# A new list of work and a finer planner's clock for a fused attention and maxout kernel

## Chip, cores and metric

The kernel runs on one core of a Trainium2 chip. The metric is the device time of one execution in microseconds (us): before, 318.02 us, the median of three runs (317.68 to 318.27).

## What is computed

Two stages in one program. First an attention through 32 inducing vectors, for four batches of 12544 rows of 128; then a maxout layer over all 50176 rows: two products to 1024 columns, their elementwise maximum, and a product back to 128.

```python
def mab(q, kv):
    s = scale * (q @ kv.transpose(0, 2, 1))
    s = s - s.max(-1, keepdims=True)
    a = np.exp(s)
    a /= a.sum(-1, keepdims=True) + 1e-09
    return a @ kv
h = mab(I, x)              # I: inducing, (B, 32, 128); x: (B, 12544, 128)
x2 = mab(x, h)             # (B, 12544, 128), then flattened to (50176, 128)
h1 = x2 @ w1               # 128 x 1024
h2 = x2 @ w2
out = np.maximum(h1, h2) @ w_out   # 1024 x 128
```

## The kernel before

**The algebra.** max(h1, h2) is h1 + relu(h2 - h1). The second attention's output is e2 times h, divided by a denominator per row, so both products are folded into the 32-row h: `hwd` is h times (w2 - w1) and `m1` is h times w1 times w_out. What is left per row is e2 (32 exponentials), a product of e2 with `hwd` (contraction over 32), a relu, a product of the relu with w_out (contraction over 1024, eight pieces of 128) and a product of e2 with `m1`, summed in the same PSUM bank; the eviction divides by the denominator.

**Tiling.** A batch has 98 chunks of 128 rows. A block is four quarters (one for each group of 32 rows of the TensorE array) of up to four chunks, 28 blocks in all. A quarter gives 2 x width units; a unit is 512 columns of relu. A quarter's chunks are also one output group, 108 in all, each with a PSUM bank while it is summed.

**Modes of TensorE.** It works in three ways: full (128 x 128: final matmuls with w_out at L932, small products), row (four tiles of 32 rows: units and the linear term, L1085) and column (four tiles of 32 columns: staging at L657, pooled scores at L356, pooled sums at L414).

**The list of work.** Every engine's order is written out by hand (`tc.manual_schedule`). `ORDER` (L1113) is a list of words, executed one after the other when the program is built:

- `pN.F`: a row phase (L1031) of up to N units, of different quarters, plus one group's linear term if N is under 4 and one is due; each unit's relu is then evicted by ACT (L1102) or by DVE (L1105), whichever would end first by the planner's clock; a bit of F turns the choice round for one unit
- a number: so many final matmuls (L920), in the order of the groups; with a group's last one the group is evicted (L954) by DVE, or chunk by chunk by ACT where `EVICT` has a 1, and stored on SP's queue (L989)
- `s`: the next block is staged (L643): its exponentials e2, evicted by ACT (L669)
- `xB.j`: a DMA transpose of a piece of batch B (L205), on SP; `gK`: a DMA transpose of block K's e2 on SP, and its denominators summed and inverted on POOL (L703); a block whose turn has not come by its first final gets its denominators by small matmuls instead (L749, L764)
- `cB.u`, `tB.u`, `aB.u`, `rB`: batch B's scores with the inducing vectors (ACT's exp, L369), their transpose on SP (L395), and the weighted sums (L398); the last `a` issues the loads of the next batch on POOL (L195)
- `eB`, `hB`, `wB`, `mB`: the small products to h, `hwd` and `m1` of batch B
- `H1`, `W`: second half of batch 0's `hwd`, and w1 times w_out

**The planner's clock.** `Clock` (L21) follows the engines with fixed durations while the list is executed. It picks the PSUM bank that comes free first (L172), the engine of a relu, and whether to put warming matmuls ahead of a wait (L879). It does not run on the chip.

**The head.** Batch 0 is loaded in twelve parts, transposed on TensorE, scored and summed in the order of `HEAD` (L814). The difference w2 - w1 is taken in three pieces (L572), w1 is cast to f16 in two halves (L576) and transposed on TensorE (L585).

**Tiles.** PSUM banks are tiles of a pool with a tag for each bank (L172); the relus have two buffers a quarter (L746), outputs six buffers (L957).

Of the kernel before, what the change touches and what calls it, by code (L numbers as in the profile page):

```python
# [20 lines left out]
class Clock:  # L21


    PAIR = 0.0558
    SWITCH = {"full": 0.11, "row": 0.097, "col": 0.097}
    LAT = 0.20
    ROW = 0.224
    SEM = 0.05

    def __init__(self):  # L30
        self.pe = self.act = self.dve = self.sp = 0.0
        self.pool = self.loading = self.loaded = 0.0
        self.stored = [0.0] * NOUT
        self.issue, self.tile = 0.0, [0.0] * 4
        self.mode = "full"
        self.bank = [0.0] * 8
        self.idle = {}
        self.log = []
        self.busy = {}
# [7 lines left out]
    def run(self, us, mode="full", ready=0.0, why="data"):  # L47
        if mode != self.mode:
            self.pe += self.SWITCH[mode]
            self.busy["sw"] = self.busy.get("sw", 0) + self.SWITCH[mode]  # L50
            self.mode = mode
# [5 lines left out]
    def on_act(self, ready, us, tail=0.12):  # L57
# [3 lines left out]
    def on_dve(self, ready, us, tail=0.085):  # L61
# [3 lines left out]
    def on_sp(self, ready, us=1.33):  # L65

        start = max(self.sp, ready)
        loading = start < 41.0 or self.loading - 1.0 < start < self.loaded - 1.0
        self.sp = start + us + (2.0 if loading and us > 1.5 else 0.0)
        late = 0.0  # L70
        if start < 42.0:
            late = 39.5 + 0.35 * (start - 27.85)
        elif start > self.loading - 1.0:
            late = min(start + 8.6, self.loaded + 4.7)
        return max(start + us + 2.4, late)
# [56 lines left out]
def kernel(  # L132
# [28 lines left out]
    relup = ctx.enter_context(tc.tile_pool(name="relup", bufs=2))  # L161
    outp = ctx.enter_context(tc.tile_pool(name="outp", bufs=NOUT))
# [7 lines left out]
    uid = [0]  # L170

    def bank(shape, dtype=F32, only=None):  # L172
        i = min(range(8), key=lambda j: ck.bank[j]) if only is None else only
        uid[0] += 1
        return i, psum.tile(shape, dtype, name=f"ps{uid[0]}", tag=f"bank{i}", bufs=1)
# [14 lines left out]
    def load_x(b, i, after=None):  # L190
# [5 lines left out]
        if b:  # L196
            if i == 0:
                ck.loading = ck.pe
            ck.on_pool(ck.pe, 0.55)
            st[b]["ld", i] = ck.loaded = ck.pe + 8.0 + 2.75 * i if b > 1 else 26.2 + 2.5 * i  # L200
# [4 lines left out]
    def transpose_x_dma(b, j):  # L205
# [3 lines left out]
        landed = ck.on_sp(st[b]["ld", i], 1.7 if n == 7 else 2.6)  # L209
# [4 lines left out]
    head16 = relup.tile([128, 4096], F16, name="head", tag="relu3")  # L214
# [10 lines left out]
    wf = relup.tile([128, 4096], F16, name="wf", tag="relu0").bitcast(F32)  # L225
    w1f, w2f = wf[:, 0:J], wf[:, J : 2 * J]
    w1s = relup.tile([128, 4096], F16, name="w1s", tag="relu1")
# [7 lines left out]
    repd = consts.tile([128, 128], F32, name="repd")  # L235
    pace = consts.tile([128, 1], F32, name="pace")

    with tc.manual_schedule(engines={ET.PE, ET.DVE, ET.Activation, ET.Pool, ET.SP}):

        xf = relup.tile([128, 4096], F16, name="xf", tag="relu2")[:, 0 : 256 * P1].bitcast(F32)  # L240
# [14 lines left out]
        nc.gpsimd.dma_start(out=woutp, in_=moe_w_out.rearrange("(jb j) c -> j jb c", j=128))  # L255
        nc.vector.memset(warm, 0.0)
# [9 lines left out]
        LANDED = [0.0, 7.58, 9.72, 11.95, 13.05, 14.12, 16.27, 17.37, 18.31, 18.94, 19.26, 19.57]  # L266
# [20 lines left out]
        def p1_scores(b, i):  # L287
# [14 lines left out]
            else:  # L302
                at = 1024 + 2 * M * (i % 2)
                et = head16[:, at : at + 2 * M].rearrange("p (k m) -> p k m", m=M)
            nc.scalar.activation(out=et[:, 0:n, :], in_=ps[:, 0 : n * M], func=AF.Exp, scale=scale)
            ck.bank[bi] = ck.on_act(end, 0.05 + n * M / 1200.0)
            st[b]["et", i] = et, ck.bank[bi]

        def p1_accum(b, i, lo=0, hi=P1):
# [4 lines left out]
            if b == 0:  # L314
                last = i == len(parts[0]) - 1
                ck.wait(ready, "p1")
                for j in range(lo, hi, 4):
                    m = min(4, hi - j)
                    nc.tensor.matmul(  # L319
                        out=st[0]["eps"][0 : m * M, 0:1],  # L320
                        lhsT=et[:, j : j + m, :].rearrange("p k m -> p (k m)"),
                        rhs=ones16[:, 0:1],
                        start=(i == 0 and j == 0),
                        stop=(last and j + m == n),
# [10 lines left out]
                st[0]["end"] = ck.run(0.0285 * (hi - lo) + 0.015 * ((hi - lo + 3) // 4))  # L335
# [866 lines left out]
```

## Time and profile before

| what | value |
| --- | --- |
| median of three runs | 318.02 us |
| the profiled execution: its own time | 317.76 us |
| its span, first to last instruction | 316.0 us |
| granted TensorE clock | 0.998 |
| final matmuls L932 | 3136, 203.5 us busy |
| row matmuls L1085 | 1262 |
| relus on ACT (L1102), on DVE (L1105) | 470 and 314, 241.0 and 199.7 us busy |
| evictions on DVE (L964) | 103, 66.0 us busy |
| last TensorE instruction ends at | 312.93 us |
| DMA, share of 16 engines: SP's and other hardware queues, POOL's | 55.8%, 22.4% |

Busy time of a matmul is modelled and overlaps that of the next; where the text speaks of what a matmul costs, it is the interval from its start to the start of the next instruction. "Issue" as a releaser means that the profile shows nothing that was waited for. The profile is of one execution, so sums are made against its own 317.76 us.

### The profile page before, as it was taken

The numbers are of one execution on the slowest core, as the hardware profiler recorded it, in microseconds if no ns is written. First come the engines' busy times: TensorE is split into PE (matmuls) and PEld (weight loads), VectorE is DVE, ScalarE is ACT, GpSimd is POOL, SyncE is SP. The second block draws the span as 40 slices with busy tenths as digits, with TensorE's granted clock in tenths as the row PEclk, the third lists the DMA queues.
The fourth block names the chain that finished last, engine by engine and source line by source line (L and its number), as shares of the span: only waits on it lengthen the run. The fifth ranks groups of instructions, "written<-read, shape, count | busy, mean of one in ns | idle before, by whom it ended". The sixth has DMA issues, their size and how long they took to land.

```text
span 316.0 us, 12577 instructions
## 1 busy us (share of the span) xinstructions
PE 308.6 (98%) x5308; PEld 239.9 (76%) x5308; DVE 274.5 (87%) x488; ACT 280.2 (89%) x580; POOL 125.8 (40%) x187
## 2 busy tenths in 40 slices
PE   6998999999999999999999999999999999999996
PEld 3885777777877777778877787887868777788885
DVE  2468999999878999988999899989899889999885
ACT  3669999999999999998999989899999999998891
POOL 7363060666620066067510064674406564461500
PEclk9999999999999999999999999999999999999999
DMA  8999999989799999898499999897323233324232
GB/s 203 208 252 205 207 219 146 207 229 230 127 218 245 245 183 174 190 233 207 121 225 252 213 227 215 204 174 203 106 85 118 100 106 118 119 88 140 102 120 101
DMA packets 81336, 55.81 MB, mean 177 GB/s; under 512 B 62816, under 2 KB 66176, under 8 KB 81280
## 3 DMA queue, kind: packets, MB, share of 16 engines
q1 hardware_dynamic: 75312, 41.32, 55.8%
q0 software_dynamic: 5968, 13.70, 22.4%
q8 instruction: 41, 0.67, 0.9%
q14 instruction: 15, 0.12, 0.1%
HBM read 27.28 MB, written 25.69 MB: 168 GB/s over the span
## 4 chain that ended last, share of the span: by engine, by line
PE 94%; DMA 2%; ACT 1%; DVE 1%; issue 1%; POOL 0%; POOLq 0%
PE ps L932 60%; PE ps L1085 23%; DMA xn<-in_x_dram 2%; PE ps L657 2%; PE ps L356 2%; PE ps L414 2%; PE ps L276 1%; PE ps L328 1%; PE ps L292 1%; PE ps L521 0%; DVE relu L1105 0%; PE ps L319 0%; ACT e L669 0%; DVE o L964 0%; ACT e_first L696 0%
## 5 line engine op out<-in xcount | busy, mean ns | idle before, releaser
L1102 ACT ACTIVATE relu<-ps 128x512 f16<-128x512 f32 x470 | 241.0, 627 | 17.5 <-PE ps L1085 16.5
L1105 DVE TENSOR_SCALAR relu<-ps 128x512 f16<-128x512 f32 x314 | 199.7, 684 | 20.6 <-PE ps L1085 19.0
L932 PE MATMUL ps<-woutp,relu 128*128 128x128 f16 x3136 | 203.5, 219 | 0.2
L932 PEld LDWEIGHTS <-relu 128*128 128x128 f16 x3136 | 176.6, 98 | 34.4 <-issue 28.7
L1085 PE MATMUL ps<-e,hwd 32*128 32x512 f16 (+2 forms) x840 | 82.8, 361 | 0.1
L720 POOL TENSOR_TENSOR half<-ed 128x256 f32<-128x256 f16 (+2 forms) x23 | 14.1, 613 | 145.8 <-DMA ed<-e 145.8
L724 POOL TENSOR_TENSOR rd<-den,minus 128x16 f32<-128x16 f32 (+2 forms) x23 | 60.7, 2639 | 1.8
L964 DVE TENSOR_TENSOR o<-ps,rd 128x512 f32<-128x512 f32 (+3 forms) x83 | 53.2, 643 | 3.9 <-PE ps L1085 2.8
L1085 PE MATMUL ps<-m,e 32*128 32x128 f16 x372 | 36.8, 216 | 0.0
L1085 PEld LDWEIGHTS <-hwd 32*128 32x128 f16 x880 | 26.7, 91 | 12.8 <-issue 3.8
L1085 PEld LDWEIGHTS <-e 32*128 32x128 f16 x372 | 22.4, 92 | 10.4 <-issue 2.7
L720 POOL TENSOR_TENSOR half<-half 128x32 f32<-128x32 f32 (+3 forms) x69 | 22.3, 323 | 5.4
L195 POOL DMA_DIRECT2D xn<-in_x_dram x32 | 17.6, 563 | 5.7 <-DMA xn<-in_x_dram 4.3
L280 DVE COPY xT<-ps 128x512 f16<-128x512 f16 (+3 forms) x12 | 5.7, 485 | 8.6 <-PE ps L276 8.6
L964 DVE TENSOR_TENSOR o<-ps,rp 128x512 f32<-128x512 f32 (+3 forms) x20 | 12.8, 642 | 0.0
L369 ACT ACTIVATE eu<-ps 128x512 f16<-128x512 f32 x18 | 11.0, 617 | 0.6 <-PE ps L356 0.3
L669 ACT ACTIVATE e<-ps 128x512 f16<-128x512 f32 (+2 forms) x21 | 11.1, 607 | 0.3 <-PE ps L657 0.2
L283 ACT COPY xT<-ps 128x768 f16<-128x768 f16 (+3 forms) x10 | 5.7, 574 | 4.3 <-PE ps L276 4.2
L276 PE MATMUL ps<-identity,xn 128*128 128x128 f16 x98 | 7.6, 220 | 1.4 <-DMA xn<-in_x_dram 0.9
L657 PE MATMUL ps<-xT,hT 128*32 128x512 f16 (+3 forms) x110 | 8.1, 361 | 0.1
L276 PEld LDWEIGHTS <-xn 128*128 128x128 f16 x98 | 5.5, 97 | 2.9 <-DMA xn<-in_x_dram 1.2
L356 PE MATMUL ps<-xT,inducingT 128*32 128x512 f16 x72 | 6.8, 386 | 0.0
(110 smaller groups left out, 117.7 us busy)
## 6 DMA issues: line engine op xcount, KB each, us to landing
out_dram<-o SPq DMA_DIRECT2D x90, 256.0 KB, 3.0
xn<-in_x_dram POOLq DMA_DIRECT2D x24, 448.0 KB, 10.4
out_dram<-o SPq DMA_DIRECT2D x10, 128.0 KB, 2.9
wf<-in_moe_w_dram POOLq DMA_DIRECT2D x4, 256.0 KB, 6.0
xn<-in_x_dram POOLq DMA_DIRECT2D x4, 224.0 KB, 10.2
xT<-xn SPq DMA_TRANSPOSE x33, 4.4
xf<-in_x_dram SPq DMA_DIRECT2D x1, 512.0 KB, 3.7
xf<-in_x_dram SPq DMA_DIRECT2D x1, 384.0 KB, 4.2
```

What stands on the lines that cost most here:

```text
L195: nc.gpsimd.dma_start(out=xn_at[b, i][:, 0:n, :], in_=xr[b, :, k0 : k0 + n, :])
L276: nc.tensor.transpose(ps[:, j, :], xn[:, g + j, :], identity16)
L356: nc.tensor.matmul(out=ps[32 * g : 32 * (g + 1), :], lhsT=inducingT, rhs=xT_tiles[b % 2][:, U * u + 4 * g : U * u + 4 * (g + 1), :], start ...
L657: nc.tensor.matmul(out=ps[32 * q : 32 * (q + 1), 128 * t : 128 * (t + n)], lhsT=hq, rhs=xT[:, c : c + n, :], start=True, stop=True, tile_p ...
L669: nc.scalar.activation(out=blk.e2[:, 0 : 128 * wd], in_=ps[:, 0 : 128 * wd], func=AF.Exp, scale=st[0]["rs"] if blk.b == 0 else scale,)
L720: nc.gpsimd.tensor_tensor(out=dst, in0=cur[:, :, 0:n], in1=cur[:, :, n : 2 * n], op=ALU.add)
L724: nc.gpsimd.tensor_tensor(out=rp[:, 0:wd, :].rearrange("p t q -> p (t q)"), in0=den[:, 0 : 4 * wd], in1=minus1[:, 0 : 4 * wd], op=ALU.pow,)
L932: nc.tensor.matmul(out=g.ps[:, 128 * c : 128 * (c + 1)], lhsT=g.blk.relu[g.q][:, 128 * (jb * w4 + t) : 128 * (jb * w4 + t + 1)], rhs=woutp ...
L964: nc.vector.tensor_mul(osb[:, 0:m, :], g.ps[:, 0 : m * C].rearrange("p (s c) -> p s c", s=m), g.blk.rp[:, t0 : t0 + m, q : q + 1].broadcas ...
L1085: nc.tensor.matmul(**seq.pop(0))
L1102: nc.scalar.activation(out=dst, in_=src, func=AF.Relu)
L1105: nc.vector.tensor_scalar(out=dst, in0=src, scalar1=0.0, scalar2=None, op0=ALU.max)
```

## The change

The list of work is another, and the relu of each unit now names its engine. The planner's clock gets other durations and more detail. The order in which the head's transposes, scores and sums run, and the order of the loads among themselves, stay; some of the small work between them moves:

- `ORDER` and `EVICT` are new. In `pN.V` a bit of V now means DVE, no bit ACT. `H` is the second half of `hwd` alone, the new word `V` holds all transposes of w1 and their copies (their first half stood ahead of the list, their second in `H`). There is a word `nK` for finals in column mode; the list does not use it.
- A unit is given only when the piece of `hwd` that it needs has been issued.
- Columns 256 to 512 of w2 - w1 move from DVE to POOL, between the loads of batch 1; the second half of w1's cast moves from ACT to POOL.
- The denominators of batch 0's pooling are summed over pieces of 4, 4, 3, 3 chunks in place of 4, 4, 4, 2, and the two last parts of two chunks together.
- Seven transfers of a few bytes from the second part of x to an unused corner of a relu buffer are issued on SP behind the loads.
- The PSUM banks are slices of one tile, the relus of a quarter slices of one tile, the outputs slices of one tile.

```diff
 class Clock:
-    PAIR = 0.0558
-    SWITCH = {"full": 0.11, "row": 0.097, "col": 0.097}
+    PAIR = 0.0563
+    COLS = 0.0566
+    SWITCH = {
+        "full": {"row": 0.095, "col": 0.095},
+        "row": {"full": 0.082, "col": 0.088},
+        "col": {"full": 0.1, "row": 0.094},
+    }
+    STEP = 0.0035
 ...
-    ROW = 0.224
+    ROW = 0.2226
 ...
+    psall = psum.tile([128, 8, 512], F32, name="psall", tag="psall")
+    relus = [big.tile([128, 2, 4096], F16, name=f"relus{q}", tag=f"relus{q}") for q in range(4)]
+    relu1 = [big.tile([128, 1024], F16, name=f"relu1_{q}", tag=f"relu1_{q}") for q in range(2)]
+    osbs = big.tile([128, NOUT, 4, C], F32, name="osbs", tag="osbs")
 ...
+        for i, k in enumerate((8, 12, 14, 15, 4, 2, 1)):
+            nc.sync.dma_start(out=probe[0:k, 16 * i : 16 * i + 8 + i], in_=xn_at[0, 1][0:k, 0, 0 : 8 + i])
 ...
+        SUMS = {14: ((0, 4), (4, 4), (8, 3), (11, 3)), 7: ((0, 4), (4, 3)), 6: ((0, 3), (3, 3)), 4: ((0, 4),)}
 ...
-        for i in range(7):
-            if i == 3:
-                difference(nc.gpsimd, 512, J, 22.4, 1.2)
+        load_x(1, 0)
+        difference(nc.vector, 0, 256, 21.0, 0.34)
+        difference(nc.gpsimd, 256, 512, 21.0, 0.64)
+        load_x(1, 1)
+        load_x(1, 2)
+        difference(nc.gpsimd, 512, J, 22.9, 1.25)
+        cast_w1(1)
+        for i in range(3, 7):
             load_x(1, i)
-        difference(nc.vector, 0, 256, 21.0, 0.3)
         sums = small_h(0)
-        difference(nc.vector, 256, 512, 21.0, 0.3)
-        weights_2(0)
 ...
-        cast_w1(1)
-        weights_2b(0)
 ...
             unit = blk.units[q][u]
+            if ("hw", ((unit[3] + 1) * (4 // unit[2]) - 1) // 2) not in st[blk.b]:
+                return None
 ...
-                if (max(ck.act, ready) + 0.477 <= max(ck.dve, ready) + 0.597) != bool(flip >> k & 1):
+                relu_out(q, blk, unit, bi, ready, bool(vector >> k & 1))
```

The list, old and new:

```diff
-s p4.13 s H1 W g2 p4.1 p2 8 m0 4 p3 p2.1 10 p3 p2 13 p3.2 6 p4.5 22 p2 p4.8 17 x1.0 p4.8 4 g1 11
-p4.1 13 p4.9 p1 16 p3.4 p2 14 p4.10 6 x1.1 4 x1.2 x1.3 x1.4 x1.5 x1.6 2 p3.6 s s s s 6 g3 6 p4.5
-14 x1.7 1 x1.8 p4.8 19 p4.10 p2.1 12 x1.9 5 p3 14 p4.4 c1.0 15 p1 p4.5 14 p4.3 g4 13 p4.8 25 p4.6
-p3.2 10 x1.10 17 p2 p3.1 15 c1.1 p4.2 12 t1.1 2 p3 6 p4.2 4 g5 11 c1.2 c1.3 p4.1 18 p4.4 t1.3 21
-p3.5 p3 22 c1.4 p1.1 p4.1 19 p2 p4.8 5 g6 21 p4.2 p2 c1.5 19 r1 a1.1 p3.2 p4 t1.5 19 a1.3 p4.9
-p2.2 29 p3.3 p4 26 p4.1 a1.5 5 p3.1 p2.3 1 e1 11 p4.12 1 h1 17 w1 s s s s p3.2 19 m1 15 p4.6 p3.6
-30 p3.1 p3.3 24 p3 p3.3 27 p3.2 p3.1 20 p4.3 p2 15 s p4.1 18 p2.1 p3 15 g7 g8 7 p3.3 p4.2 9 g9 12
-x2.0 3 x2.1 x2.2 s p1.1 p4.4 x2.3 12 p4.5 14 p4.6 14 p4 14 p3 21 p3.6 p4.8 14 g10 4 x2.4 4 x2.5
-x2.6 9 p4.13 s c2.0 14 p4.6 p1 5 x2.7 4 x2.8 13 p3.3 p3.4 23 p4.4 11 c2.1 p4 p1 9 t2.1 4 g11 x2.9
-4 x2.10 10 p4.3 p3 15 c2.2 p3.3 21 p3.1 p3.5 27 p3.3 p3.2 c2.3 19 p4.10 4 g12 4 t2.3 5 p4.1 17
-p3.1 p3.4 16 a2.1 c2.4 p3.1 p3.1 23 p4.4 18 p2.1 p4.9 13 g13 17 p4.9 p3.3 24 a2.3 c2.5 p4.1 p2 7
-t2.5 12 r2 18 p3 p4.2 30 p4.10 p2.2 16 a2.5 p4.3 p3.6 8 e2 10 p4.2 2 h2 21 p3.1 p3.6 11 w2 4 m2
-15 p4.11 s s s 13 p3 p2 12 s p4 15 p2 p3.2 22 p3.5 p3.2 3 x3.0 4 x3.1 19 p3.4 p4.12 25 p3.3 13 p3
-p3.3 27 p3.2 p3.5 12 g15 8 g14 3 p4 11 s s p3.1 p2.2 14 x3.2 4 x3.3 4 x3.4 x3.5 5 p3.1 p4.5 19
-x3.6 17 p3.4 p4.1 23 g16 14 p4.4 p3 27 c3.0 s p3.1 15 x3.7 c3.1 p4.2 p1 x3.8 15 p4.4 21 p3.4 p3 8
-g17 14 p3.3 p2 6 t3.1 12 p4.2 p1 20 p3.4 p3.4 22 p4.10 p2.1 30 p4.3 p3 4 g18 8 x3.9 4 x3.10 7
-c3.2 a3.1 c3.3 p4.3 p2 9 t3.3 15 p4.4 17 p2.1 p4.8 27 p2.2 p4.1 13 g19 18 p3.3 p4.4 10 r3 8 c3.4
-c3.5 a3.3 p4.5 20 t3.5 1 p4.8 p2.2 21 p4.4 13 p3.5 p2 1 g20 27 p4.4 p3.3 27 a3.5 p4.8 p2.3 2 e3
-16 h3 14 p3.5 p4.2 10 w3 4 m3 15 s p4.1 9 g21 10 p3.1 p2.1 15 p3.5 s s s 13 p3.1 p3.4 22 p4.8 p1
-27 p4.3 p3 9 g22 13 p2.2 p2 22 p3.2 p4.3 25 s s p3.4 13 p3 p3.3 30 p4.9 p3.2 g23 21 p4.2 20 p4.1
-p2.2 30 p3.4 p4.2 24 s p2 p3.2 12 p4.8 g24 22 p4.6 p2.2 20 p2.1 p3.2 16 p3.1 p2 11 p4.9 21 p4.3 9
-p1 p3 g25 p1 20 p3.1 p3.4 30 p4.8 p3.1 26 p4.8 13 p4.6 13 p4.3 9 g26 13 p3.3 p3 27 p3.5 p2 22 p2
-p4.1 22 p2.2 p4.9 22 p3 p2.1 g27 27 p4.1 p3.2 38 p4.3 p3.1 31 p2 p4.9 22 p2.1 p3.1 24 p3 p4.11 40
-p3.4 p3 21 p4.6 21 p2.1 p3.4 31 p4.4 p4.3 63
+s p4.9 s p2.2 H1 V W p2.2 p4.2 14 m0 p3.1 4 p3.2 4 p3.3 15 p4.2 6 x1.0 2 p3.6 15 p4.8 13 p4.5 14
+p3.1 x1.1 10 p1 p4.6 14 p4.1 20 p4.5 p2.2 16 s x1.2 s p3.5 15 p4.1 g3 18 g4 p3.4 p2.1 x1.3 11
+x1.4 p4.5 14 p4.1 14 p3.3 10 p4.5 s c1.0 18 p2.1 g5 p3.1 x1.5 x1.6 6 x1.7 6 p4.9 11 x1.8 12 p3.6
+p3.4 17 s c1.1 p3.4 12 x1.9 3 p4.12 3 x1.10 4 p3.2 11 p4.1 21 p4.2 p2.1 21 p4.6 t1.1 12 p1 p4.5
+14 c1.2 c1.3 p4.10 23 p3.2 t1.3 p3.2 23 p4.3 18 p2.1 p4.8 28 p4.12 p2 23 g6 p4.5 a1.1 c1.4 a1.3
+c1.5 p3.4 11 r1 t1.5 14 p4.8 p3.2 31 p2.1 p4.4 9 a1.5 p4.8 5 e1 17 h1 5 p4.3 p3.1 21 w1 6 s s
+p4.10 25 p3.1 p3.4 33 p4.3 p3.1 24 s s p3.4 18 p2.2 p4.2 11 m1 13 p3.4 4 p4.12 21 p1 p3.2 15 p2.2
+p4.2 18 p4.5 15 p1.1 p4.2 x2.0 x2.1 14 x2.2 3 p4.5 6 x2.3 13 x2.4 p4.4 p2.1 14 g9 9 x2.5 p3.6 p2
+13 p4.9 21 p2.2 p4.2 31 x2.6 x2.7 p3.5 p4.1 26 x2.8 g10 c2.0 s p4.12 21 p2.1 p4.8 23 p4.3 10 p3.3
+c2.1 s c2.2 13 p3.1 7 t2.1 1 p4.3 8 x2.9 2 g11 x2.10 g12 4 p4.3 16 p4.8 13 p4.12 15 p3.2 15 c2.3
+p3.4 p3.1 28 p3.4 p3.4 22 p4.5 13 s t2.3 c2.4 a2.1 c2.5 p3.1 p3.1 21 g13 7 p2.1 t2.5 p4.2 28 p2.1
+p4.10 6 r2 22 p3.6 p3 24 p4.1 a2.3 a2.5 p3.2 5 p4.6 14 p4.1 e2 24 p4.3 p3 12 h2 19 p4.1 p2.1 18
+p4.10 10 p3.4 12 w2 6 p4.14 s s s 23 p2.2 p4.1 24 p3.6 s p3.2 14 p4.8 8 m2 6 p4.4 23 p3.1 p2.2 12
+g17 2 x3.0 g15 p4.8 21 p2.1 x3.1 x3.2 p4.8 29 p3.1 x3.3 p4.10 24 p3.4 11 p4.9 x3.4 13 p4.4 16
+p4.10 21 p3.1 p3.2 11 x3.5 x3.6 g1 g16 10 p4.1 x3.7 21 p2.1 p4.1 31 p3.2 p4.3 29 p4.5 10 x3.8
+p3.5 s s c3.0 c3.1 13 p4.12 18 p3.3 p2 2 t3.1 9 x3.9 x3.10 3 p4.1 18 p3.5 p3 27 p4.9 p2.1 19 s
+c3.2 c3.3 a3.1 p4.10 p2.1 19 g19 t3.3 g18 p4.9 5 r3 16 p3.1 p3.1 20 p4.5 21 p3.2 p3.2 31 p4.14 p3
+27 p4.12 a3.3 c3.4 c3.5 11 p3.3 p3 8 t3.5 23 g20 p4.8 p3.3 31 p2.1 p4.8 23 p4.6 a3.5 p1 p3.4 10
+p4.1 2 g7 1 e3 10 g14 7 h3 6 p4.3 p3.2 14 w3 3 m3 5 s s s 11 g21 p1 p4.4 21 p4.10 12 p1 p4.6 15
+p4.8 19 p2.3 p4.2 28 g23 p2.2 p4.2 19 p3.4 3 g22 19 p3.2 p4.6 39 p3.1 p3.2 31 p4.10 p3.2 31 p4.3
+p2 22 p4.5 11 p3.1 8 p4.1 17 p4.10 14 p3.6 s s s 11 p4.2 8 p3.5 14 g24 p4.1 16 p4.9 12 p4.1 p1.1
+g8 23 p4.14 p2 15 s p4.1 21 p4.8 p2.1 30 g27 p4.2 p3.5 20 g26 p4.1 18 g25 3 p2.2 p4.1 31 p3.3
+p4.4 28 p4.12 p1 17 p4.3 18 p2.2 p4.8 31 p3.4 p4.6 1 g2 30 p2.2 p4.8 31 p3.1 p4.5 32 p4.5 p2 30
+p4.10 p2 24 p4.8 p2.1 32 p3.6 p3.1 23 p2.3 p4.1 36 p2.1 p3.1 24 p4.1 p4.7 56
-EVICT = "000000000000000000000000101000000000000000000000010000000000000000000010000000000000000000000000000000010000"
+EVICT = "000000000000000000000000000000000000000000000000000000000000000000000000000000000000000000000000000000101101"
```

## The prediction

> **What bounds the kernel now.** I read the page's totals and its chain by engine first, then the waits between 28 and 313 us.
>
> ```profile
> span 316.0 us, 12577 instructions
> ...
> PE 308.6 (98%) x5308; PEld 239.9 (76%) x5308; DVE 274.5 (87%) x488; ACT 280.2 (89%) x580; POOL 125.8 (40%) x187
> ...
> PE 94%; DMA 2%; ACT 1%; DVE 1%; issue 1%; POOL 0%; POOLq 0%
> ```
>
> ```profile
> PEld L932 <- issue: 28.7, 105, 0.8
> DVE relu L1105 <- PE ps L1085: 18.5, 56, 0.9
> ACT relu L1102 <- PE ps L1085: 16.5, 46, 0.9
> ```
>
> The chain is TensorE's own program. ACT and DVE wait for TensorE 16.5 and 18.5 us, and TensorE waits for nobody by name; its losses stand under "issue", where a change of mode and a wait for a bank look alike. The timeline of TensorE separates them.
>
> ```profile
> 44.42 1.01 PE L932 MATMUL ps<-woutp,relu 128*128 128x128 f16 x15
> ...
> 45.37 0.56 PE L1085 MATMUL ps<-e,hwd 32*128 32x512 f16 x4
> ...
> 95.69 1.68 PE L932 MATMUL ps<-woutp,relu 128*128 128x128 f16 x27
> ...
> 97.24 0.68 DVE L964 TENSOR_TENSOR o<-ps,rd 128x512 f32<-128x512 f32 x1
> ...
> 97.43 0.92 PE L1085 MATMUL ps<-e,hwd 32*128 32x512 f16 x4
> ...
> 98.28 0.23 PE L932 MATMUL ps<-woutp,relu 128*128 128x128 f16 x1
> ```
>
> Fifteen final matmuls start at 44.42 and the next kind at 45.37: 0.95 us, that is 15 at 0.056 and 0.11 for the change of mode. At 97.31 a row run starts (matmuls of L1085) and the next final comes at 98.28: 0.97 us, where the run at 95.15 gave way after 0.54. The 0.43 between is a stall: the bank was freed by the eviction on DVE that began at 97.24.
>
> So the program has a bill (matmuls and changes of mode) and stalls on top, and I price the change on both.
>
> **The bill.** The list of work has a word per step: pN is a row phase of N units, digits are final matmuls, s, c and a are column work (staging, scores, sums), the rest is small. Taking the start of each run of one mode to the start of the next in TensorE's timeline of before: the 151 row runs take 74.9 us together; the 53 of one phase 0.34 each on average (0.326 at best), the 97 of two phases 0.58 (0.54 at best), of which the 30 that pair a p4 with a p1 or p2 take 0.56 and the others 0.59. Counted in the two lists:
>
> - Row runs: 250 phases in 151 runs become 242 in 164: 86 of one phase, 78 of two, 39 of them a p4 with a p1 or p2. 86 x 0.34 + 39 x 0.56 + 39 x 0.59 = 74.1 us, against 74.9: **-0.8**.
> - Full runs: 151 become 160, each ending in one change of about 0.10: **+0.9**. The 3136 finals and the small products of each batch stay.
> - Column runs: 33 become 24. A lone staging step takes 0.33 and four in one run 0.905 (42.30 to 43.2), so a lone one pays 0.33 - 0.905/4, about 0.11. Nine at 0.11: **-1.0**.
> - Denominators: in the old list blocks 0, 1, 7, 8 and 14 have no turned e2 when their first final comes and take four small matmuls each (L764 x20). In the new one the word g2 stands behind block 2's finals too: 4 more at 0.025 = **+0.1**, and one DMA transpose and one chain on POOL fewer, both hidden.
>
> Sum of the bill: -0.8. ACT and DVE keep their load: the masks behind the dots name 311 units for DVE and leave 473 to ACT (now 314 and 470), and four groups' evictions are on ACT in place of five. At the very end the last one-chunk group moves from DVE (0.286 us) to ACT (0.376): 0.1 at most, left out.
>
> **The head.** The seven probe transfers stand on SP behind the loads of x and wait for a landing at 9.74; SP has no other work until its first transpose at 25.59, so they cost nothing. Without that cover seven issues of some 0.5 us (a store's, 71.99) would hold back the first transpose by 3.5, and it is block 2's, which the new list no longer needs. The denominators' sums change from pieces of 4, 4, 4, 2 to 4, 4, 3, 3, as many matmuls, and the last four chunks need one in place of two (0.13 us each in the chain before 21.5). What follows is this chain:
>
> ```profile
> 22.57 0.84 ACT e_first L696 x2
> 23.41 0.51 ACT w1s L582
> 23.91 0.59 ACT e L669
> 24.50 0.49 ACT relu L1102
> 24.99 0.58 ACT e L669
> 25.56 0.48 ACT w1s L599
> ```
>
> W's second half on TensorE (L607) starts behind it, at 26.09.
>
> The cast L582 goes to POOL: -0.51 on ACT's queue. But p4.9 leaves two relus to ACT where there was one, and p2.2 adds one ahead of V and W: +0.98. The copy L599, and with it W on TensorE, comes some 0.5 later, with two more units already issued; behind it stand p2.2 p4.2 and 14 finals, against p4.1 p2 and 8. Two units and the finals moved forward are worth about what the delay costs. I take 0; bounds -0.6 (cast and one sum saved, delay covered) and +0.8 (delay of 0.5 and the cast late on POOL). POOL's cast is not in the trace: between L720's 128x256 (0.665) and L573's 128x512 (1.27); behind L573, which ends at 24.24, it ends by 25.5, ahead of ACT's copy. Behind it wait the loads 3 to 6 of batch 1, issued about 1.3 later; the first three alone land until 31.74, so the transfers stay fed.
>
> The subtraction of columns 256 to 512 leaves DVE (0.42 at 21.86) for POOL, where half of L573 is 0.64. It is due at 22.55 (second L521), and its weights land at 20.98: ends by 21.7, hidden. The Trainium skill, SBUF — State Buffer, "SBUF: two separate sides", says that a DVE instruction with two SBUF inputs and a GpSimd instruction that reads SBUF hold their shared ports exclusively, one blocking the other. Both subtractions now wait for the same landing; if POOL goes first, DVE's first one ends at 20.98 + 0.64 + 0.43 = 22.05 in place of 21.41, and hT (L473, 21.66) comes 0.39 later: the sum would be 0.4 higher. No stretch of this trace has such a pair, so it cannot be told here.
>
> **The stalls.** Row runs above their best sum to 74.9 - 70.3 = 4.6 us (53 x 0.326 + 97 x 0.54 + 0.68 = 70.3); the new mix at old averages leaves 74.1 - 70.2 = 3.9. What sets them is where the planner thinks each engine is. Its old constants charge 0.11 for the way back to full mode and 0.224 for a phase; from the start of a phase's last matmul to the next final it is 0.304 at most returns without a stall, which the new constants (0.2226 and 0.082) give exactly. Over 142 returns the old plan runs TensorE late by 142 x 0.028 = 4 us, so the real TensorE comes to banks earlier than planned. DVE and ACT relus repeat at 0.598 to 0.608 and 0.477 to 0.493; old constants are at the low end (0.597, 0.477), new ones in the middle. ACT idles 18.8 and DVE 24.7 us after 29 us, so there is slack to be placed better. I take two fifths of 3.9 off: **-1.6**. Bounds: -3.9 (all gone) and +3 (a plan whose units collide elsewhere, as many stalls again as are left over).
>
> The changed tiles (all banks one tile, relus one per quarter) keep the same buffers; a wait more per instruction would have to show as stalls and lies in the same bounds.
>
> **Sum.** -0.8 + 0 - 1.6 = -2.4. The profiled execution took 317.76 (span 316.0 and 1.76 around it): 315.4. The median of the three runs, 318.02, is 0.26 above it: **315.6**. Bounds: -0.8 - 0.6 - 3.9 gives 312.7, -0.8 + 0.8 + 3 gives 321.0.
>
> **Rivals.**
> 1. *The stalls keep their averages; the constants do not matter.* For it: old stalls are already small, 0.03 us a run. Against: they are uneven, 0.43 and 0.24 in single runs. -0.8 alone: 317.2.
> 2. *The plan fits and almost nothing stalls.* For it: slack on ACT and DVE. Against: 93 and 91% busy there. -0.8 - 0.4 - 3.7: 313.1.
> 3. *The last sum of batch 1 waits for its transpose.* Adding the bill word by word, c1.5 to a1.5 was 9.0 us and is now 5.7. In the trace c1.5's scores start at 73.52, their transpose is issued at 77.94, behind a store and a transposed e2 on SP's queue, and lands at 82.62, 9.1 later; a1.5 starts at 82.80. If it takes as long again, TensorE stands 9.1 - 5.7 = 3.4 us before a1.5, with the next batch's h, hwd and staging behind it. For it: the tightest cover of the list. Against: without a queue the way is 0.33 + 0.2 + 0.62 (exp) and 3.1 to 4.9 to land, 4.3 to 6.1. Place: between c1.5 and a1.5; 315.6 + 3.4 = 319.0; it decides from 3.1 us of wait on.
> 4. *Nothing changes*: the mix brings nothing, the head costs its 0.8: 318.0.
>
> **How the numbers follow.** A measurement of this kernel tells some 0.2% (0.64 us) from no change: 317.4 to 318.7 is the same. Forecast 0.36, rival 1 0.18, rival 2 0.14, rival 4 0.10, rival 3 (and stalls near their upper bound) 0.22. Rival 1 lies just past the edge and gives a little to "same": faster 0.65, same 0.12, slower 0.23. The likeliest case's own range is 314.3 to 316.8. The range 312.7 to 319.5 reaches over rivals 2, 1, 4 and most of 3.
>
> **What would show it.** After: 164 row runs, 160 full, 24 column runs, L764 x24, POOL's pow x22. Row runs near 72.5 us if the stalls shrink as forecast, near 74.1 for rival 1. A gap before the sums' weight loads near 82 us, released by the DMA of eT, for rival 3. In the head: start of W's second half at 26.1 (before) against 26.6, and DVE's subtraction longer than 0.43 if the ports clash. I am wrong if row runs take over 75 us, or if a wait longer than 1 us appears that the old trace has not.

## The result, and the profile after

The changed kernel takes 316.19 us, the median of ten runs (314.63 to 317.26); beside it the kernel before took 317.82 (317.65 to 318.27). The ratio is 0.9941, with a 95% interval of 0.9923 to 0.996. That is 1.6 us less, 0.8 less than forecast in the difference and well inside the range. The profiled execution took 315.13, 2.63 less than the one profiled before. Most of the gap between these two figures goes with TensorE's clock: five of the ten runs have a mean granted clock of 0.993 to 0.995 and average 316.60, the other five (0.998 and 1.0, the profiled one among them) average 315.36.

First the page after: span, totals and the chain by engine.

```profile
span 313.3 us, 12580 instructions
...
PE 306.2 (98%) x5310; PEld 239.7 (76%) x5310; DVE 273.4 (87%) x485; ACT 280.9 (90%) x581; POOL 122.4 (39%) x183
...
PE 89%; DMA 6%; ACT 2%; DVE 1%; SPq 1%; issue 1%; POOL 0%; POOLq 0%
```

The waits between 28 and 313 us (engine, line and tile, what was waited for: total us, times, longest):

```profile
PEld L979 <- issue: 28.0, 112, 0.4
...
DVE relus L1091 <- PE psall L1154: 15.4, 45, 1.1
ACT relus L1094 <- PE psall L1154: 14.8, 39, 0.9
```

ACT and DVE do the same work as before; the span is 2.7 shorter, and they wait 1.7 and 3.1 us less for TensorE. DMA's share of the chain rose from 2% to 6%: two transposes stand in it now, and TensorE waits for each, by 0.2 to 0.3 us (both are told under rival 3).

Where the time went, by TensorE's modes. Each run of one mode is taken from its start to the start of the next, from 8.5 us to the last matmul (so one run of row mode in the head, in both, is counted too):

| mode | before: runs, us | after: runs, us | difference |
| --- | --- | --- | --- |
| row | 152, 75.52 | 165, 72.65 | -2.87 |
| full, with the last run | 153, 211.16 | 162, 212.21 | +1.05 |
| column | 34, 17.74 | 25, 16.74 | -1.00 |
| last TensorE instruction ends | 312.93 | 310.20 | -2.73 |

The three differences sum to -2.82; the rest is a start 0.09 later. The row runs' excess over their best (0.326 for one phase, 0.540 for two) fell from 4.78 to 1.95 us, by the lists' own count: 53 runs of one phase and 98 of more before, 86 and 78 after, and the one in the head taken at 0.540 in both. 35 runs lost more than 50 ns each, now 13 do. The best of the two mixes is then the same, 70.74 and 70.70 us, so 2.83 of the row runs' 2.87 us are stalls that went.

By place: the first row run of real work starts at 22.90 in place of 23.44 (-0.54); from there to the 100th final it takes 15.14 in place of 13.86; from the 100th final to the end of TensorE 272.16 in place of 275.63 (-3.47). The two lists have different work ahead of the 100th final, so the middle figure is not a loss by itself: its 1.28 is, to within 0.1, row matmuls with 0.83 more (12 runs in place of 9) and the transposes of w1 with W, 0.50 more (eight transposes stand behind the first row run, where there were four). In the latter is a wait. The timeline around W, before and after (start, us, engine, line and operation, and in brackets idle time and what ended it):

```profile
24.73 0.39 PE L607 MATMUL ps<-woutp,w1s 128*128 128x128 f16 x4
26.09 0.40 PE L607 MATMUL ps<-woutp,w1s 128*128 128x128 f16 x4 [0.98 <-ACT w1s L599]
```

```profile
24.07 1.28 DVE L1091 TENSOR_SCALAR relus<-psall 128x512 f16<-128x512 f32 x2
...
24.53 0.74 PE L634 MATMUL psall<-identity,relus 128*128 128x128 f16 x8
...
25.27 0.74 DVE L573 TENSOR_SCALAR hwd<-psall,rs 128x512 f16<-128x512 f32 x1
25.61 0.62 ACT L642 COPY relus<-psall 128x512 f16<-128x512 f16 x1
25.93 0.41 DVE L639 COPY relus<-psall 128x512 f16<-128x512 f16 x1
26.39 0.62 PE L651 MATMUL psall<-woutp,relus 128*128 128x128 f16 x8 [1.12 <-DVE relus L639]
```

From the last transpose of w1 (25.05) to W (26.39) TensorE starts nothing for 1.34 us. ACT's copy of w1 has ended at 26.23; DVE's, behind its relus and `hwd`, at 26.34, and that one releases W. Before, the wait was 1.20 long and lay inside W, between its halves (24.90 to 26.09), so the new one is only 0.14 longer.

### The profile page after: what moved, and what is told of

Read it like the earlier page. It is cut to its first block, busy times and chain, and to the rows that moved or that the text cites. A ratio compares the mean times of both kernels' runs of the same rounds, so it can differ in the third digit from the quotient of the medians.

```text
span 313.3 us, 12580 instructions
## 1 busy us (share of the span) xinstructions
PE 306.2 (98%) x5310; PEld 239.7 (76%) x5310; DVE 273.4 (87%) x485; ACT 280.9 (90%) x581; POOL 122.4 (39%) x183
## 4 chain that ended last, share of the span: by engine, by line
PE 89%; DMA 6%; ACT 2%; DVE 1%; SPq 1%; issue 1%; POOL 0%; POOLq 0%
PE psall L979 58%; PE psall L1154 21%; DMA xn<-in_x_dram 2%; PE psall L701 2%; DMA xT<-xn 2%; DMA eT<-eu 2%; PE psall L312 1%; PE psall L461 1%; PE psall L402 1%; ACT relus L1094 1%; PE psall L374 1%; PE psall L328 1%; SPq L241 1%; DVE relus L1091 1%; PE psall L569 1%
## 5 line engine op out<-in xcount | busy, mean ns | idle before, releaser
L1094 ACT ACTIVATE relus<-psall 128x512 f16<-128x512 f32 x468 | 239.2, 619 | 15.9 <-PE psall L1154 14.8
L1091 DVE TENSOR_SCALAR relus<-psall 128x512 f16<-128x512 f32 x308 | 195.5, 683 | 16.7 <-PE psall L1154 15.8
L979 PE MATMUL psall<-woutp,relus 128*128 128x128 f16 x3104 | 203.9, 220 | 0.0
L979 PEld LDWEIGHTS <-relus 128*128 128x128 f16 x3104 | 174.9, 98 | 33.5 <-issue 27.7
L1154 PE MATMUL psall<-e,hwd 32*128 32x512 f16 (+2 forms) x840 | 81.1, 362 | 0.0
L1014 DVE TENSOR_TENSOR osbs<-psall,rd 128x512 f32<-128x512 f32 (+1 forms) x80 | 50.9, 637 | 4.6 <-PE psall L1154 1.6
L1154 PE MATMUL psall<-m,e 32*128 32x128 f16 x372 | 36.6, 216 | 0.0
L765 POOL TENSOR_TENSOR half<-half 128x32 f32<-128x32 f32 (+4 forms) x66 | 21.4, 324 | 5.2
L1014 DVE TENSOR_TENSOR osbs<-psall,rp 128x512 f32<-128x512 f32 (+3 forms) x24 | 15.6, 649 | 0.5 <-PE psall L1154 0.4
L714 ACT ACTIVATE e<-psall 128x512 f16<-128x512 f32 (+2 forms) x21 | 10.9, 574 | 0.1
```

The lines of the kernel that those rows point to most:

```text
L714: nc.scalar.activation(out=blk.e2[:, 0 : 128 * wd], in_=ps[:, 0 : 128 * wd], func=AF.Exp, scale=st[0]["rs"] if blk.b == 0 else scale,)
L765: nc.gpsimd.tensor_tensor(out=dst, in0=cur[:, :, 0:n], in1=cur[:, :, n : 2 * n], op=ALU.add)
L979: nc.tensor.matmul(out=g.ps[lo:hi, 128 * c : 128 * (c + 1)], lhsT=relu[:, lo:hi], rhs=woutp[:, jb, :], start=not g.started, stop=(state["m ...
L1014: nc.vector.tensor_mul(osb[:, 0:m, :], g.ps[:, 0 : m * C].rearrange("p (s c) -> p s c", s=m), g.blk.rp[:, t0 : t0 + m, q : q + 1].broadcas ...
L1091: nc.vector.tensor_scalar(out=dst, in0=src, scalar1=0.0, scalar2=None, op0=ALU.max)
L1094: nc.scalar.activation(out=dst, in_=src, func=AF.Relu)
```

## The experiments

Each kernel is the changed one with one edit. A ratio is against the kernel before, run beside it; "body" is the time from the 100th final to the end of TensorE in the profile, 275.63 before (276.20 in a second profile) and 272.16 after (272.20 in a second).

**Which part holds the gain.** The old list, with each unit's engine as the old planner had chosen it, in the changed kernel:

```diff
-        s p4.9 s p2.2 H1 V W p2.2 p4.2 14 m0 ...
+        s p4.14 s H1 V W g2 p4.9 p2 8 m0 ...
```

> The new kernel with the old list of work: each unit's relu on the engine that the old planner chose, old evictions; head, tiles, probes and planner's durations stay new. Theory (the list holds the gain of the row runs): 151 row runs take 74 to 75.5 us again, the first row run stays at 22.9, the time is about 0.5 us under before: 317.3, ratio 0.998. Rival (the banks that the new durations pick, or the new tiles, took the stalls away): row runs at 72 to 73, time 316.0 to 316.4.

It took 318.81 us, ratio 1.0023 (1.0007 to 1.0039). Row runs 75.74 us with an excess of 5.0, body 275.52: both the old kernel's figures. So the list with its named engines holds the whole gain of the body, and the changed tiles and the piece of `hwd` that a unit waits for cost nothing there. The new durations, which stay and pick the banks, bring nothing with the old list. The time was expected at 317.3, with the first row run at 22.9; in the profile that run starts at 24.21. The page's row of the granted clock (40 slices, tenths of full speed) shows a part of the reason:

```profile
span 318.5 us, 12583 instructions
...
PEclk9977999999999999999999999999999999999999
```

Two stretches ran at half clock; in 5 of its 12 runs the mean clock was 0.995 or less. It is not all: the other seven, at 0.999 or 1.0, take 318.13 to 318.82, 318.55 in the middle, where the kernel before took 318.25 beside them. In the profile a gap in the head of 1.05 us is in it too (the last section); what else the head lost in this list was not tried.

The small work of the head put back (differences, cast of w1, as before):

```diff
-        load_x(1, 0)
-        difference(nc.vector, 0, 256, 21.0, 0.34)
-        difference(nc.gpsimd, 256, 512, 21.0, 0.64)
-        ...
-        cast_w1(1)
-        for i in range(3, 7):
+        for i in range(7):
+            if i == 3:
+                difference(nc.gpsimd, 512, J, 22.4, 1.2)
             load_x(1, i)
+        difference(nc.vector, 0, 256, 21.0, 0.3)
         sums = small_h(0)
+        difference(nc.vector, 256, 512, 21.0, 0.3)
 ...
```

> The new kernel with the small work of the head where it was: columns 256 to 512 of w2 - w1 on DVE, the second half of w1's cast on ACT, the loads of batch 1 as before; the list stays new. Theory (the head's 0.5 us come from this work): first row run at 23.4 in place of 22.9, row runs stay at 72.0, 316.7, ratio 0.9965. Rival (the half microsecond is lost again behind W or won elsewhere in the head): the time stays within 0.3 of the new kernel's 316.2.

316.38 us, 0.9939 (0.9921 to 0.9958): what the changed kernel itself took. The first row run starts at 23.86, near the 23.4 of the theory, but for another reason: x lands 0.41 later here and the sums end 0.6 later still, with the gap that the last section tells. Moving the small work was worth nothing that could be measured. From the last of the pooled sums to the first row run it is 1.9 to 2.0 us in both.

The denominators' pieces put back to 4, 4, 4, 2, and one matmul for each of the last parts:

```diff
-                if n > 2:
-                    cuts = [(et, j, m) for j, m in SUMS[n]]
-                else:
-                    cuts = [(pair16, 0, 4)] if last else []
+                cuts = [(et, j, min(4, n - j)) for j in range(0, n, 4)]
 ...
```

> The new kernel with the denominators' sums of batch 0 over the old pieces (4, 4, 4, 2 chunks, the last two parts each by itself). Theory (the new pieces are what brings the first row run forward, 0.13 us for each large part, and what brings TensorE to its 450th instruction before that has arrived): from the landing of the last part of x to the end of the sums 1.8 to 1.9 us in place of 1.40 to 1.45, first row run at 23.3 to 23.5, and the gap at the 450th instruction about 0.4 us shorter than in the new kernel (0 to 0.4 where the sixth part of x lands at 16.3 to 16.6); the time is 0 to 0.4 us over the control, 316.4 to 316.8. Rival (the moved subtraction and cast bring the head forward): the sums end as early as in the new kernel, first row run at 22.9 to 23.1.

317.09 us, 0.9959 (0.9944 to 0.9974). The time from the landing of x's last part to the start of the last sum: 19.58 to 21.45, 1.87; the changed kernel has 19.52 to 20.92, 1.40 (1.43 in its second profile), the old one 1.80 and 1.91. So most of the head's gain of half a microsecond is the sums'; the first row run starts at 23.32. TensorE's timeline of this kernel shows the price, two changes between the sums' small matmuls and the weighted sums at the very end of the load:

```profile
21.02 0.19 PE L362 MATMUL psall<-ones,relus 128*64 128x1 f16 x1
21.14 0.21 PE L371 MATMUL psall<-relus,xn 128*128 128x32 f16 x2
21.29 0.19 PE L362 MATMUL psall<-ones,relus 128*64 128x1 f16 x1
21.41 0.21 PE L371 MATMUL psall<-relus,xn 128*128 128x32 f16 x2
...
26.82 0.94 PE L648 MATMUL psall<-woutp,relus 128*128 128x128 f16 x8 [1.52 <-DVE relus L636]
```

and after, the same place:

```profile
20.75 0.20 PE L374 MATMUL psall<-relus,xn 128*128 128x32 f16 x2
20.85 0.18 PE L365 MATMUL psall<-ones,relus 128*128 128x1 f16 x1
20.89 0.20 PE L374 MATMUL psall<-relus,xn 128*128 128x32 f16 x2
```

Its median is not the sums alone: W waits 1.74 us here (25.08 to 26.82) and 7 of its 8 runs show the half-clock stretch; the eighth took 315.93.

The seven probe transfers left out:

```diff
-        for i, k in enumerate((8, 12, 14, 15, 4, 2, 1)):
-            nc.sync.dma_start(out=probe[0:k, 16 * i : 16 * i + 8 + i], in_=xn_at[0, 1][0:k, 0, 0 : 8 + i])
```

> The new kernel without the seven probe transfers. Theory (hidden, SP has nothing else to do): first row run at 22.9, time as the new kernel, 316.2, within 0.3. Rival (they delay the loads of x or the first transposes): 0.3 to 1.0 us faster, 315.2 to 315.9.

315.44 us, 0.9917 (0.9884 to 0.9949). The middle is 0.8 us below the changed kernel's, but the intervals overlap (0.9923 to 0.9949); whether the probes cost something stays open.

**The row runs.** 24 pairs of row phases pulled apart, the same finals around them:

```diff
-p4.8 p3.2 31
+p4.8 2 p3.2 29
```

> The new kernel with 24 pairs of row phases torn apart by two finals each, so 24 more row runs and 24 more full runs with the same matmuls. Theory (a bill by runs: two single row runs 2 x 0.326 against one double 0.54, and one more change out of a full run at 0.10): 24 x 0.21 = 5.0 us more, 321.2, ratio 1.010. Rival (the changes fill time in which TensorE would wait anyway): less than 2 us more, under 318.2.

320.04 us, 1.0051 (1.0032 to 1.007). The body is 276.79, 4.63 longer than after: 0.19 for each split, of which one half is in the row runs (74.95 against 72.65 us) and the other in the other modes, the way to full mode and back. The prediction's prices give 2 x 0.34 - 0.58 + 0.10 = 0.20, the theory's 0.21. The bill's unit price stands. (The profiled run carries a half-clock stretch too, from 28.45, ahead of the body.)

Each unit's engine chosen while the program is built, by the new durations, in place of the named one, from the 200th final on:

```diff
-relu_out(q, blk, unit, bi, ready, bool(vector >> k & 1))
+relu_out(q, blk, unit, bi, ready, max(ck.act, ready) + 0.484 > max(ck.dve, ready) + 0.604 if state["done"] >= 200 else bool(vector >> k & 1))
```

> The new list in its order, but after 200 final matmuls each relu goes to the engine that would end first by the planner's new durations, as the old kernel chose; 357 of 784 relus change their engine (334 on DVE in place of 311). Theory A (the stalls went because the list names the engine of each relu): the row runs stall 3 to 4.5 us again and the time is 2 to 3 us over the new kernel, 318.5. Theory B (the order of the words did it): row stalls stay under 2 us and the time within 0.5 us of 316.4.

325.65 us, 1.0244 (1.0206 to 1.0281): far over both theories. 357 of the 784 relus change engine, though DVE ends with 334, few more than the 311 named ones. Row runs take 80.37 us, the excess is 9.68 in place of 1.95, and ACT waits for TensorE's units longer:

```profile
PEld L979 <- issue: 36.0, 124, 0.7
ACT relus L1094 <- PE psall L1154: 30.3, 62, 1.9
DVE relus L1091 <- PE psall L1154: 11.0, 34, 1.1
```

So in this order the engines named in the list cannot be left to the rule: choosing the one that ends first, unit by unit, costs some 9 us (body 281.37). That is no price for naming an engine as such. The kernel before did not follow the bare rule either: 271 bits in its list turn the choice round, which the theory here leaves out. A new choice of engines for the old order was not tried.

**The wait in W and the clock.** The changed kernel once more:

> The new kernel itself, as the control of this call. Expected: ratio 0.994 to the kernel before; about half of its runs with a mean granted clock of 0.993 to 0.995 and about 1.5 us longer than those at 0.998 to 1.0; the kernel before stays at 0.998 to 1.0 in nearly all runs.

316.53 us, 0.9953 (0.9937 to 0.997). Of its 12 runs six show a mean clock of 0.993 to 0.995 and take 316.71 to 317.40; the others, at 0.999 or 1.0, take 315.31 to 316.36. The kernel before shows such a clock in none or one of the runs beside each experiment, out of 13 to 18.

Five matmuls on zeros ahead of W, so that TensorE isn't idle there:

```diff
             ck.wait(max(ck.bank[bi], w_of["w1T"]), "w")
+            for _ in range(5):
+                nc.tensor.matmul(out=ps, lhsT=warm[:, 0:128], rhs=warm, start=True, stop=True)
             for jb in range(NJB):
```

> The new kernel with five matmuls on zeros (128 x 512, 0.216 us each) in the 1.3 us in which TensorE waits ahead of W; nothing else differs. Theory (the idle time ahead of W makes one 3.4 us window of the head idle enough that the clock is halved in the next one, which costs about 1.6 us where it happens): nearly all runs at 0.998 to 1.0, the time as in the undisturbed runs of the control, 1.0 us under its median: 315.1, ratio 0.991. Rival (the lower clock has nothing to do with the wait ahead of W): the share of runs at 0.993 to 0.995 and the median stay as in the control, 316.2.

315.27 us, 0.9922 (0.9896 to 0.9947). Four of its six runs have the full clock, at 315.05 to 315.31; two don't, and the profiled one shows that its half-clock stretch is at another place, 17.35 to 20.76. So the theory's nearly all runs at full clock came out for four of six.

W put behind the two row phases:

```diff
-s p4.9 s p2.2 H1 V W p2.2 p4.2 14 m0 ...
+s p4.9 s p2.2 H1 V p2.2 p4.2 W 14 m0 ...
```

> The new kernel with W behind the next two row phases (V p2.2 p4.2 W in place of V W p2.2 p4.2). Theory (the wait ahead of W is for DVE's copy, which stands behind three relus and hwd; the row phases need hwd alone, ready 0.3 us sooner): the row run starts at 26.0 to 26.1 in place of 26.95, W waits for nothing, 0.3 to 0.5 us gained in the undisturbed run, and fewer runs at a lower clock since less is idle: 315.3 to 315.9. Rival (the finals behind are late anyway): 316.2 as the control.

315.29 us, 0.9921 (0.9891 to 0.9951). All six runs have the full clock. But the wait only moved: the units stand for `hwd` as long. Counted from the first row run, which starts at 23.76 here, they come 0.89 us earlier, as the theory had it, and yet the 100th final comes no sooner: 15.25 after that run, against 15.14 in the changed kernel. The median is about the mean of the changed kernel's runs at full clock (315.36).

```profile
25.08 0.61 PE L634 MATMUL psall<-identity,relus 128*128 128x128 f16 x8
26.92 0.50 PE L1154 MATMUL psall<-e_first,hwd 32*128 32x128 f16 x10 [1.24 <-DVE hwd L573]
```

The warming matmuls and no probes:

> The five matmuls ahead of W, and the seven probe transfers left out. Theory (the probes cost nothing): as the run with the five matmuls alone, within 0.3 us, 315.1. Rival (the probes cost something, since leaving them out alone measured 315.44): 0.5 to 0.8 us under it, 314.4.

314.66 us, 0.9901 (0.9876 to 0.9927), all six runs at 0.999 or 1.0. That is 0.6 under the run with the matmuls alone, as the rival has it, but these intervals overlap too.

```profile
span 312.7 us, 12568 instructions
...
PEclk9999999999999999999999999999999999999999
```

The same with the word r3 (the scores of batch 3's last rows, which need the last transpose of x, L427) moved behind t3.5:

> The new kernel with five matmuls on zeros ahead of W, without the probes, and with r3 behind t3.5 (nine row phases later). Theory (r3 waits 0.2 to 1.2 us for the transpose of x3.10 where it stands): that wait is gone, TensorE's time from its 100th final to its end is under 271.5 (271.65 to 272.4 without it), 314.3, ratio 0.989. Rival (the wait falls on a3.5 in place of r3): 314.7 as without the move.

315.04 us, 0.9898 (0.9872 to 0.9923). The wait at r3, 0.3 us in the changed kernel, is gone, and the body is 271.70 against 271.65 without the move: no further gain, and above the 271.5 of the theory. With the move and without it, the middle is below both the kernel before and the changed one; against the second set of the changed kernel (0.9937 at its lower end) the intervals are apart, against the first they still touch.

The kernel before, as a control and for a second profile:

> The kernel before once more, for a second profile of it. Theory (in the head TensorE stands at its 450th instruction because its next instructions arrive late; the old head reaches that point some 0.4 us later than the new one): the gap there is 0 to 0.9 us where the new kernels show 0.25 to 1.35, mean clock 0.998 to 1.0. Rival (only the new head has it): no gap there whenever the sixth part of x lands at 15.2 to 15.5.

318.02 us, 0.9996 (0.9979 to 1.0012); body 276.20, row excess 5.35, and no gap, with the sixth part landing at 16.25.

## Why the prediction came out right, step by step

- **The sum.** Forecast -2.4 against the profiled execution, -2.63 there. The medians differ by 1.6, since about half of the changed kernel's runs have the lower clock and take 1.24 us longer in the mean (1.10 in the second set), a step that the prediction does not have. Its terms were near or off in both directions, and that they cancel so well is in part luck.
- **The bill, -0.8.** Run counts came as read: 164 row runs besides the one in the head, L808 x24 where L764 had 20, 22 chains on POOL. Column runs -1.00 (forecast -1.0). Full runs +1.05 (forecast +0.9 and +0.1), but that figure came out in part by luck: 0.44 of a gap in the head (below), 0.14 of W and 0.34 of r3 are in it, and shorter sums, some 0.45, against it. What is left for nine more runs and four small matmuls is some 0.6, not 1.0, though a change does cost what was forecast where it was measured alone (the split pairs). Where the other 0.4 went was not found.
- **The stalls, -1.6.** The direction was right, the size too small. The row runs' bill of -0.8 held 0.7 of stalls already (4.6 to 3.9), so the forecast had them fall by 2.3 in all; they fell by 2.83, half of the 3.9 in place of two fifths. The best of the mix did not change, as forecast. That the plan and the named engines set these stalls, rather than averages that stay (rival 1) or other parts of the change, is shown by the old list (5.0) and by the engines chosen afresh (9.68). The reason that the prediction gives, better durations, is not shown: with them in place the old list kept its stalls and the choice unit by unit had nearly twice as many, so they can have acted only through the list that was written with them. One reading behind that reason was too neat as well. Of the 88 returns before whose last row matmul has 512 columns, 47 take 0.303 to 0.31 us and 40 take 0.31 to 0.32; 0.304 is the lower of two values, so the 4 us by which the old plan is said to run late are rough.
- **The head, 0.** The first row run came 0.54 earlier, inside the bounds, but the steps were not those forecast. The sums' new pieces gave 0.4 to 0.5 us, where the prediction had one matmul of 0.13; the moved small work, the cast's 0.51 with it, gave nothing. W starts at 26.39, near the 26.6 forecast, but by another chain: I had ACT's copy last, and it was DVE's (26.34 against 26.23). The subtraction on POOL ended at 21.92, 0.2 later than forecast, and hid all the same.
- **Port clash.** The two subtractions started 0.12 us apart:

```profile
21.03 0.89 POOL L616 TENSOR_TENSOR w<-relus 128x256 f16<-128x256 f32 x1 [0.58 <-DMA relus<-in_moe_w_dram]
```

 DVE's took 0.42 from 20.91, as ever. POOL's took 0.89, where the same instruction takes 0.72 or 0.73 in the three profiles in which DVE's does not overlap it (the old list, the warmed W, the kernel with r3 moved); half of the 512-column form, 0.64, was an estimate too low. In two other profiles POOL went first, without the probes (21.20 against 21.23) and with W moved (21.12 against 21.24): there DVE's took 0.97 and 0.95. So both orders occur, and the later one is the longer; only in the split pairs, 0.01 apart, did POOL's, the first by the profile, take 1.01. That is what the Trainium skill, SBUF — State Buffer, "SBUF: two separate sides", says: whichever starts first holds the shared ports, and the other waits. In the changed kernel's two profiles DVE won. Where POOL did, hT started 0.42 and 0.43 behind the last sum, in the changed kernel's profiles 0.28 and 0.33, before 0.22, so the price of the clash was 0.1 to 0.2, not 0.4.
- **Rival 3, 3.4 us before a1.5.** It did not happen. The scores of c1.5 start at 77.42 and a1.5 at 83.17, 5.75 later as counted, with no gap ahead of it. The transpose is issued at 78.57, 1.15 behind the scores, where it was 4.4 before: the short queue on SP, which I had put against the rival, decided. The transpose in the chain ("DMA eT<-eu", 5.41 from 71.51) is that of the sum before, a1.3, which starts 0.46 behind the matmul ahead of it, against 0.20 or 0.21 in seven other profiles: some 0.25 lost. A second wait for a transpose appeared at a word I had not looked at, r3:

```profile
205.51 0.45 PE L979 MATMUL psall<-woutp,relus 128*128 128x128 f16 x5
206.08 0.11 PEld L427 LDWEIGHTS <-xT 128*128 128x128 f16 x2 [0.29 <-DMA xT<-xn]
```

 From start to start it is 0.34; 0.49 in the second profile, 0.06 to 1.35 in the others, so it varies with when the transfer lands.
- **Rivals 2 and 4.** Almost no stalls (313.1) would have left 0.2 of the excess and my own case 2.3; 1.95 is left. Nothing (318.0) is excluded by the interval.

## What to carry to other kernels

Price a reordered list on two accounts. The bill (runs of each mode by their best durations) can be read off the list, and held to 0.01 us for each run split off here (0.19 against 0.20). Stalls depend on where each engine stands, so they come with the order and the engines together: neither averages of the old list nor, in this order, a rule that picks the engine that ends first (9 us dearer) gave them. After such a change look at the head's waits again: one of 1.20 us and one of 1.34 look alike in the chain, but around them may lie a whole window in which TensorE is half idle, and the runs with the lower clock took 1.24 and 1.10 us more in the mean of the two sets. A few matmuls on zeros in such a wait went with 3 such runs of 17, where 11 of 22 had it.

## What the runs showed of the hardware

**One window at half clock.** Each stretch at half clock inside the work is 3.41 us long (the old list has two, from 17.53 and from 27.77). The busy time of the engines in the window ahead and in the one itself, without the probes:

```profile
25.23:28.64 3.41, 1.84 (x37) 1.36 (x35) 2.30 (x5) 2.48 (x6) 1.69 (x4) 1.00 1.06 211
28.65:32.06 3.41, 3.41 (x34) 2.25 (x32) 2.45 (x6) 2.85 (x7) 0.00 (x0) 0.50 1.06 211
```

and in the changed kernel, where none followed:

```profile
24.20:27.61 3.41, 2.17 (x34) 1.43 (x34) 2.30 (x5) 2.49 (x6) 2.72 (x6) 1.00 1.07 200
27.62:31.03 3.41, 3.39 (x55) 2.34 (x54) 3.37 (x8) 3.41 (x8) 0.00 (x0) 1.00 1.07 210
```

The columns are the stretch, its length, busy time and instructions of PE, PEld, DVE, ACT and POOL, the granted clock, DMA's share and GB/s. With PE busy 1.66 (the old list), 1.84, 1.89 (old sums) and 1.90 us (split pairs) of 3.41, half clock followed; with 2.17 it did not. It is not that share alone: in the kernel with the warming matmuls 2.23 us, of narrow matmuls of the head, were followed by half clock at 17.35, and 2.53 (the old list) and 2.59 (the kernel with r3 moved) by half clock at 17.53 and 16.94. The Trainium skill, TensorE: Matmul & The Clock Gate, "Part 1: The HAM clock gate", gives a free-running window of 3413 ns and two rates, with which these rows agree; the Trainium skill has the half rate come after an idle window, and here a window about half busy was enough. That the same kernel falls in it in half of its runs would follow from that window's phase; no run shows it, since both profiles of the changed kernel itself have the full clock.

That the wait in W is behind it is borne out by counts, not shown by a trace: with the wait as it is, 11 of 22 runs of the changed kernel have a mean clock of 0.995 or less (8 of 22 in four more kernels with that wait: without the probes, with the head's work put back, the pairs split, the engines chosen afresh), with it longer (1.74) 7 of 8, with it filled 3 of 17. W moved, 0 of 6, speaks less clearly, since there TensorE stands 1.24 us for `hwd` instead. And a second place bears on the clock: the gap that follows next. The three stretches that begin at 16.94 to 17.53 lie beside it, two of them in kernels whose wait in W is filled. Of the eleven profiles with this gap, five of the seven in which it is over 1 us have half clock ahead of 32 us, and none of the four in which it is under 0.8. The old sums, with no gap and the wait of 1.74 us, have the lower clock without it; where the wait is as it was, the two are not told apart, and a part of the time that goes with the lower clock may be the gap's.

**A gap in which the next instructions come late.** At about 16.1 us, inside the weighted sums, TensorE stops between two matmuls that wait for nothing. After, and without the probes:

```profile
16.54 0.24 PE L374 MATMUL psall<-et,xn 128*128 128x32 f16 x3 [0.27 <-issue]
```

```profile
17.34 0.24 PE L372 MATMUL psall<-et,xn 128*128 128x32 f16 x3 [0.97 <-issue]
```

From start to start it is 0.44 and 1.15 us. It is always ahead of TensorE's 450th instruction, weight loads and its sequencer's counted, in every profile of the new head but that with the old sums; it was 0.4 to 0.8 where x's sixth part lands at 16.3 to 16.6 and 1.05 to 1.39 where that lands at 15.1 to 15.5. The two profiles before have no such gap; they reach that instruction some 0.4 us later, with the sixth part landing at 16.25 and 16.36.

What TensorE most likely stands for is in the traces. The page lists a DMA queue for instructions:

```profile
q8 instruction: 41, 0.67, 0.9%
```

That is 41 packets of 16 KB. The first of them ends at 15.27 in the changed kernel's profile and between 15.12 and 16.22 in the others, and the 450th instruction starts 1.24 to 1.43 us behind that end in all fourteen profiles, those before and with the old sums too, which get there just then. So the gap is as long as TensorE is early. That match leaves little room for another cause, though nothing was changed to try it. The two groups follow as well: where that packet starts at 14.2 to 14.5, x's sixth part lands at 16.25 to 16.6; where it starts at 14.8 to 15.3, that part lands at 15.1 to 15.5, ahead of the packet's end. Which of the two goes first differs between runs; what decides it was not tried. Where the gap was short the sums still ended by the landing of x; where it was long they ended 0.6 to 1.5 us later than that allows.
